# RWKV attention and a routed MoE on one core: the scan's inputs in three loads, asked for a chunk ahead, and scaled in place

## The chip, the cores and the metric

One core of a Trainium2 chip runs the whole program. A time is what one execution takes on the device, in microseconds (us); a verdict compares medians of several executions. The engines are TensorE (PE, with its weight loads as PEld), VectorE (DVE), ScalarE (ACT), GpSimd (POOL) and SyncE (SP). Each works through its own queue of instructions in order. SP issues nearly all DMAs here, and an instruction that waits holds up all that stand behind it in its queue.

## What is computed

Two stages, one fed by the other (shapes: batch 4, 8 heads, 768 steps, head size 40, float32):

```python
for t in range(768):                     # per batch and head
    y[t]  = r[t] @ state
    Sa    = state @ a[t]                 # state is 40x40
    state = state * w[t] - outer(Sa, b[t]) + outer(v[t], k[t])
x = y, 3072 tokens of 320 numbers
e = argmax(x @ w_gate); out = gate(e) * sigmoid(x @ w_output_gate)[e] * (relu(x @ w1[e]) @ w2[e])
```

## The kernel before, in words

The 768 steps are cut into 12 chunks of 64 steps. Within a chunk the recurrence is written as matrix products and the inverse of a triangular matrix, so that only the state goes from chunk to chunk. `Att` does the attention, `Moe` the experts.

For each chunk `c` four pieces of work follow each other:

- `scan(c)` (lines 98 to 119) loads `w` (371 KB) and `D`, which holds a, k and b side by side (1080 KB), and runs two scans on DVE that give products of decays, `P` and `I`. The scans read a constant of ones and zeros, `rst`, which POOL writes (lines 77 and 78). Then a reciprocal `rq` and the scaling of `I`.
- `prep(c)` (line 126): DVE scales a into `Av` (lines 173 and 174) and k, b into `KBt` (line 190). SP copies `Av` to two places in on-chip memory, to `Am` (line 180) and to strips of `LA` (line 167); three DMAs each, 330 KB together. PE multiplies `KBt` with `Am` into `pl` (line 203). ACT and DVE move `pl` to `N` and `LA`, and POOL masks `LA` (line 218). PE transposes `KBt` and `Wp` (line 152).
- `tinv` (line 227) inverts the triangular matrices on DVE: chunk 0 and chunk 1 alone, then two chunks at a time. Its first instruction reads `N` (lines 242, 247), its last gives `Tc` (lines 306, 312).
- `crit(c, q)` (line 343), for each half `q` of the heads, is the chain that carries the state: PE products `pa` with `XS`, `Tc`, `N`, with moves on ACT and additions on DVE between them. `tail(c, q)` gives the output `x`, which `route` stores (`xd`) and multiplies with the gate.

After chunks 3, 7, 10 and 11 `pick` chooses the experts, and POOL scatters the records (`tab`, line 695), each scatter behind the last. When chunk 7 is picked, the table is read back (`tr`, `tb`, line 804), tokens are gathered (`xg`, line 745) and transposed (`px`, line 753), and the first expert starts while the attention still runs. Afterwards the experts run alone: `ph` (line 776) and `po` (lines 789 to 791).

`run` (line 473) is a program order: `crit` in front, and after each of its steps four steps of a background generator, which does `prep`, `scan` of the next chunk and `tinv`. A scheduler then reorders the instructions of each engine by its own estimate of their times; `issue_after` says that what it encloses may not be placed before a given instruction. The order that it gives is fixed in the program. The tile names are the buffers: a tile of a pool with one buffer can be written again only when all that read it are done. `Av`, `KBt`, `D` and `w` have one buffer each. At the start, 56 products with zeros (`warm`, line 121) keep PE busy. They wait for `zb`, a constant that POOL writes.

## Time and profile before

| | us |
|---|---|
| median of 3 runs | 729.64 |
| the runs | 729.64, 733.31, 726.88 |
| the profiled execution, its time | 735.93 |
| its span, first to last instruction | 734.2 |

| engine | busy us in the span | share |
|---|---|---|
| PE | 651.8 | 89% |
| PEld | 582.8 | 79% |
| DVE | 470.2 | 64% |
| ACT | 339.8 | 46% |
| POOL | 208.7 | 28% |

The mean granted TensorE clock was 0.945 of full speed. The attention takes the time up to about 470 us, with the first expert mixed in from about 400 us on; the rest is the experts. The profiled execution stands 6.29 us above the median of the runs; durations are read from it and sums are made against its 735.93 us.

### The profile page before, as it was taken

What the parts mean: (1) busy time and instruction counts of PE and PEld (TensorE: products, weight loads), DVE (VectorE), ACT (ScalarE), POOL (GpSimd) and SP (SyncE); (2) the same over time, 40 slices, a digit from 0 to 9 for tenths busy, and PEclk for the clock granted to TensorE, in tenths of its full rate; (3) what the DMA queues carried; (4) which work ended last, traced back from release to release, by engine and by line L of the source; (5) the groups of instructions that cost most, each with busy time, mean ns of one, the idle gap of its engine ahead of it and who ended that gap; (6) DMA issues with size and microseconds to landing.
All of it is one profiled execution on the core that took longest, in us unless ns stands there. A gap on an engine that the chain in (4) does not pass through costs nothing.

```text
span 734.2 us, 21196 instructions
## 1 busy us (share of the span) xinstructions
PE 651.8 (89%) x8898; PEld 582.8 (79%) x8898; DVE 470.2 (64%) x914; ACT 339.8 (46%) x781; POOL 208.7 (28%) x316
## 2 busy tenths in 40 slices
PE   6768986898999999799998599788999999999994
PEld 5557875787987888688887488678999998988994
DVE  6678679868986898797796134453575544554230
ACT  2568662674477377347633144242465333433120
POOL 8442120330322246222112100243533231402111
PEclk9777899999999999999999599988999999999998
DMA  7865552276347538532333542065385633431001
GB/s 174 178 152 138 148 141 74 72 172 147 88 133 182 117 91 182 124 94 82 84 78 76 111 134 59 21 178 165 102 226 160 180 121 104 130 117 45 18 10 30
DMA packets 64387, 85.12 MB, mean 116 GB/s; under 512 B 34586, under 2 KB 51613, under 8 KB 62846
## 3 DMA queue, kind: packets, MB, share of 16 engines
q1 hardware_dynamic: 60446, 74.79, 40.4%
q0 software_dynamic: 3840, 8.91, 4.3%
q8 instruction: 72, 1.18, 0.7%
q14 instruction: 29, 0.24, 0.1%
HBM read 67.59 MB, written 8.96 MB: 104 GB/s over the span
## 4 chain that ended last, share of the span: by engine, by line
PE 61%; DVE 13%; DMA 12%; ACT 7%; issue 4%; POOL 2%; SPq 0%; POOLq 0%; DVEq 0%; ACTq 0%
PE ph L776 14%; PE pa L368 6%; PE pM L440 5%; PE po L791 5%; PE po L789 5%; PE po L790 5%; DMA D<-in_din_dram 5%; PE pS L406 3%; PE pt L152 3%; PE pY L456 3%; PE pl L203 3%; PE pY L455 2%; ACT N L214 2%; PE pa L355 2%; PE pxt L623 2%
## 5 line engine op out<-in xcount | busy, mean ns | idle before, releaser
L218 POOL TENSOR_SCALAR_AFFINE_SELECT LA<-LA 64x192 f32<-64x192 f32 x144 | 59.3, 441 | 88.7 <-ACT LA L216 85.9
L781 DVE SCALAR_TENSOR_TENSOR hl<-ph,hh 128x480 fp32r<-128x480 f32 (+1 forms) x76 | 41.8, 563 | 66.4 <-ACT hh L780 66.3
L776 PE MATMUL ph<-xh,w1h 128*128 128x480 f32 (+1 forms) x228 | 80.5, 357 | 1.9 <-DVE hl L781 1.3
L789 PE MATMUL po<-w2h,hh 128*120 128x320 f32 x256 | 79.2, 313 | 1.0 <-ACT hh L780 0.9
L776 PE MATMUL ph<-xl,w1h 128*128 128x480 f32 (+1 forms) x228 | 79.9, 353 | 0.0
L790 PE MATMUL po<-w2l,hh 128*120 128x320 f32 x256 | 78.2, 309 | 0.0
L780 ACT ACTIVATE hh<-ph 128x480 fp32r<-128x480 f32 (+1 forms) x76 | 36.7, 498 | 86.8 <-PE ph L776 86.8
L791 PE MATMUL po<-w2h,hl 128*120 128x320 f32 x256 | 75.9, 310 | 0.0
L794 POOL DMA_INDIRECT out_dram<-y,ti x32 | 33.1, 1035 | 131.8 <-DVE y L793 69.0
L359 ACT ACTIVATE As<-pa,hq 128x320 f32<-128x320 f32 x80 | 42.1, 527 | 57.1 <-PE pa L368 48.0
L203 PE MATMUL pl<-Am,KBt 120*128 120x192 f32 (+1 forms) x288 | 59.1, 338 | 9.6 <-ACT LA L216 6.1
L456 PE MATMUL pY<-KB,M 128*64 128x64 f32 (+1 forms) x768 | 55.6, 231 | 10.9 <-DVE M L444 10.9
L214 ACT ACTIVATE N<-pl 32x192 f32<-32x192 f32 (+1 forms) x138 | 51.6, 374 | 25.7 <-PE pl L203 12.0
L695 POOL DMA_INDIRECT tab<-rec,si x24 | 28.4, 1182 | 117.6 <-DVE rec L692 46.5
L368 PE MATMUL pa<-As,Tc 64*32 64x40 f32 x1792 | 52.0, 206 | 9.4 <-ACT As L359 6.2
L456 PEld LDWEIGHTS pY<-KB,M 128*64 128x64 f32 x768 | 48.9, 144 | 13.9 <-DVE M L444 11.5
L455 PE MATMUL pY<-Sd,R 128*64 128x64 f32 (+1 forms) x704 | 56.9, 234 | 0.3 <-DVE base L669 0.3
L368 PEld LDWEIGHTS pa<-As,Tc 64*32 64x32 f32 x1792 | 41.1, 113 | 19.9 <-ACT As L359 7.3
L203 PEld LDWEIGHTS pl<-Am,KBt 120*128 120x128 f32 x288 | 44.7, 197 | 15.1 <-ACT LA L216 9.2
L440 PE MATMUL pM<-R,VU 128*128 128x128 f32 x384 | 53.8, 293 | 1.5 <-ACT VU L432 1.4
L776 PE MATMUL ph<-xh,w1l 128*128 128x480 f32 (+1 forms) x152 | 53.7, 353 | 0.0
L455 PEld LDWEIGHTS pY<-Sd,R 128*64 128x64 f32 x704 | 47.4, 143 | 4.7 <-issue 1.7
(186 smaller groups left out, 1562.2 us busy)
## 6 DMA issues: line engine op xcount, KB each, us to landing
D<-in_din_dram SPq DMA_DIRECT2D x12, 1080.0 KB
st<-in_w_dram SPq DMA_DIRECT2D x16, 512.0 KB
st<-in_w_dram SPq DMA_DIRECT2D x16, 480.0 KB
XS<-in_vt_dram SPq DMA_DIRECT2D x24, 256.0 KB
XU<-in_vt_dram SPq DMA_DIRECT2D x24, 256.0 KB
VU<-in_vl_dram SPq DMA_DIRECT2D x24, 208.0 KB
w<-in_win_dram SPq DMA_DIRECT2D x12, 371.2 KB
st<-in_w_dram SPq DMA_DIRECT2D x16, 256.0 KB
```

Source lines behind the costliest of these rows:

```text
L203: nc.tensor.matmul(pl[:, i, 0:nj], KBt[:, 6 * side + g0 + i].rearrange("p n t -> p (n t)"), Am[:, g0 + i:g0 + i + 6 * nj - 5:6, 0:64], sta ...
L214: s.mark['n', c] = nc.scalar.activation(out=nn, in_=pn, func=AF.Copy, scale=-1.0).ins
L218: g.affine_select(out=la[:, :, i], in_=la[:, :, i], pattern=[[0, nj], [1, C]], base=0, channel_multiplier=-1, compare_op=ALU.is_gt, fill=0.0)
L359: nc.scalar.activation(out=x, in_=pa, func=AF.Copy, scale=s.hq[:, h:h + 1])
L368: nc.tensor.matmul(pa[o + w:o + w + 32, i], m(p)[o:o + 64], x[o:o + 64, i, :], start=start, stop=True, tile_position=(o, o + w), skip_grou ...
L440: nc.tensor.matmul(pM[:, i], VU[:, h0 + i].rearrange("p n t -> p (n t)"), R[:, :, h0 + i], start=True, stop=True)
L455: nc.tensor.matmul(o, R[:, side, i, :], Sf[:, 40 * i:40 * i + w], start=True, stop=False)
L456: nc.tensor.matmul(o, Ms[i // 4][:, i % 4, side, :], Kf[:, k:k + w], start=not c, stop=True)
L776: nc.tensor.matmul(ph, l, r, start=(i == 0), stop=(i == 7))
L789: nc.tensor.matmul(po, hh[f][:, ts_], w2h[:, f], start=(f == 0), stop=False)
L790: nc.tensor.matmul(po, hh[f][:, ts_], w2l[:, f], start=False, stop=False)
L791: nc.tensor.matmul(po, hl[f][:, ts_], w2h[:, f], start=False, stop=(f == 7))
```

## The change

The host lays a (padded from 64 to 66 columns) and k, b in two arrays, `ain` and `kin`, where there was one. `load_w`, `load_a` and `load_k` load `w` (two buffers), `a` (371 KB, one buffer) and `kb` (720 KB, two buffers). Chunk 0's loads are issued at the start; those of chunk c + 1 are written in `prep(c)`. `Av` and `KBt` are no tiles of their own any longer: the products overwrite `a` and `kb`. `rst` is written by DVE, and first. Chunk 1's scans may not be placed before the scaling of chunk 0's `kb`, and the loads of the state, the gate's weights and chunk 2's `w` may not be placed before chunk 0's copies to `Am`.

```diff
@@ -37,14 +37,16 @@
     wd = d3([w]).reshape(nch, 120, 12, C)
     win = np.zeros((nch, 120, 12, 2, 33), w.dtype)
     win[:, :, :, 0, 1:], win[:, :, :, 1, 1:] = wd[..., 32:], wd[..., 31::-1]
-    din = np.ascontiguousarray(d3([a, k, b]).transpose(0, 1, 2, 4, 5, 3, 6)).reshape(nch, 120, 12, 3, C)
+    ain = np.zeros((nch, 120, 12, C + 2), a.dtype)
+    ain[..., 0:C] = d3([a]).reshape(nch, 120, 12, C)
+    kin = np.ascontiguousarray(d3([k, b]).transpose(0, 1, 2, 4, 5, 3, 6)).reshape(nch, 120, 12, 2, C)
     tr = lambda x: x.reshape(2, 2, 8, nch, C, 40).transpose(3, 1, 0, 5, 2, 4)
     rl = np.ascontiguousarray(tr(r))
     vl = np.zeros((nch, 2, 104, 8, C), v.dtype)
     vl[:, :, 0:40], vl[:, :, 64:104] = tr(v)[:, :, 0], tr(v)[:, :, 1]
     vt = np.ascontiguousarray(v.reshape(2, 2, 8, nch, C, 40).transpose(3, 1, 4, 2, 0, 5))
     vt = np.concatenate([vt, np.zeros(vt.shape[:-1] + (24,), vt.dtype)], -1)
-    return win, din, rl, vl, vt
+    return win, ain, kin, rl, vl, vt
 
 
 def pat(x, off, dims):
@@ -55,9 +57,9 @@
 class Att:
     npool = 0
 
-    def __init__(s, ctx, tc, ident, win, din, rl, vl, vt, nch=12):
+    def __init__(s, ctx, tc, ident, win, ain, kin, rl, vl, vt, nch=12):
         s.tc, s.nc, s.nch, s.ident = tc, tc.nc, nch, ident
-        s.win, s.din, s.rl, s.vl, s.vt = win, din, rl, vl, vt
+        s.win, s.ain, s.kin, s.rl, s.vl, s.vt = win, ain, kin, rl, vl, vt
         nc = s.nc
         pool = lambda n, b, **k: ctx.enter_context(tc.tile_pool(name=n, bufs=b, **k))
         s.cp, s.p2, s.p5 = (pool(f"p{i}", i) for i in (1, 2, 5))
@@ -65,6 +67,9 @@
         s.dr = pool("dr", 2, space=DRAM)
         s.pre = ExitStack()
         s.p1 = s.pre.enter_context(tc.tile_pool(name="p0", bufs=1))
+        s.rst = s.p1.tile([120, 792], BF16, name="rst")
+        nc.vector.memset(s.rst, 0.0)
+        nc.vector.memset(s.rst[:, 0:792:33], 1.0)
         s.mM = s.cp.tile([128, C], F32, name="mM")
         nc.gpsimd.memset(s.mM, 1.0)
         for h in range(2):
@@ -73,9 +78,6 @@
 
         s.Am = s.p1.tile([120, 2, NP, 66], F32, name="Am")
         nc.gpsimd.memset(s.Am, 0.0)
-        s.rst = s.p1.tile([120, 792], BF16, name="rst")
-        nc.gpsimd.memset(s.rst, 0.0)
-        nc.gpsimd.memset(s.rst[:, 0:792:33], 1.0)
         s.Tt = s.p1.tile([128, 1056], F32, name="Tt")
         nc.gpsimd.memset(s.Tt, 0.0)
         nc.gpsimd.memset(s.Tt[:, 0:1056:33], 1.0)
@@ -92,21 +94,33 @@
         s.zb = s.cp.tile([128, 32], F32, name="zb")
         nc.gpsimd.memset(s.zb, 0.0)
         s.buffers()
+        s.w, s.a, s.kb = {}, {}, {}
         s.st, s.ld, s.post, s.idle, s.mark = {}, {}, [], False, {}
 
+
+    def load_w(s, c):
+        n = 12 * 2 * 33
+        w = s.w[c] = s.p1.tile([120, n + 1], F32, name="w", bufs=2)
+        s.nc.vector.memset(w[:, n:], 0.0)
+        with s.tc.issue_after(s.mark['am', 0]) if c == 2 else ExitStack():
+            s.nc.sync.dma_start(out=w[:, 0:n], in_=s.win[c])
+
+    def load_a(s, c):
+        s.a[c] = s.p1.tile([120, 12, 66], F32, name="a")
+        s.nc.sync.dma_start(out=s.a[c], in_=s.ain[c])
+
+    def load_k(s, c):
+        s.kb[c] = s.p1.tile([120, 12, 2, C], F32, name="kb", bufs=2)
+        s.mark[c] = s.nc.sync.dma_start(out=s.kb[c], in_=s.kin[c]).ins
 
     def scan(s, c):
 
         nc, V = s.nc, s.nc.vector
         n = 12 * 2 * 33
-        w = s.p1.tile([120, n + 1], F32, name="w")
-        V.memset(w[:, n:], 0.0)
-        nc.sync.dma_start(out=w[:, 0:n], in_=s.win[c])
-        s.D = s.p1.tile([120, 12, 3, C], F32, name="D")
-        s.mark[c] = nc.sync.dma_start(out=s.D, in_=s.din[c]).ins
+        w = s.w.pop(c)
         P, I = (s.p1.tile([120, 12, 2, 33], F32, name=x) for x in "PI")
         Pf, If = (x.rearrange("p r h t -> p (r h t)") for x in (P, I))
-        with s.tc.issue_after(s.mark['t', 0]) if c == 2 else ExitStack():
+        with s.tc.issue_after(s.mark['t', 0] if c == 2 else s.mark['k', 0]) if c in (1, 2) else ExitStack():
             for o, d in ((Pf, w[:, 0:n]), (If[:, ::-1], w[:, n:0:-1])):
                 V.tensor_tensor_scan(out=o, data0=d, data1=s.rst, initial=0.0, op0=ALU.mult, op1=ALU.add)
         wq = pat(w, 1, [(33, 24), (1, 32)])
@@ -129,8 +143,12 @@
         g, V = nc.gpsimd, nc.vector
         st = s.st[c] = {}
         P, I, rq = s.Q
-        D = s.D
-        yield
+        a, kb = s.a.pop(c), s.kb.pop(c)
+        Av = a
+        yield
+        if c + 1 < s.nch:
+            s.load_w(c + 1)
+            s.load_k(c + 1)
         LA = st["LA"] = s.p5.tile([128, 2, NP, 66], F32, name='LA', bufs=4)
         if c:
             g.memset(LA[32:64], 0.0)
@@ -142,7 +160,6 @@
         st['Np'] = s.Np
         for h in range(2):
             g.memset(N[64 * h + 32:64 * h + 64, :, 32:64], 0.0)
-        Av = s.p1.tile([120, 12, 66], F32, name="Av")
         Wp = s.p1.tile([120, 6, 2, C], F32, name="Wp")
 
         def back(dst, src):
@@ -168,7 +185,6 @@
 
         rs = s.p1.tile([120, 24], F32, name="rs", bufs=2)
         nc.scalar.activation(out=rs, in_=rq, func=AF.Square, accum_out=s.rqm[:, c:c + 1])
-        a, kb = D[:, :, 0], D[:, :, 1:3]
         with s.tc.issue_after(s.mark['r', 0]) if c == 1 else ExitStack():
             V.tensor_tensor(out=Av[:, :, 0:33], in0=a[:, :, 0:33], in1=I[:, :, 1, ::-1], op=ALU.mult)
             V.tensor_tensor(out=Av[:, :, 33:64], in0=a[:, :, 33:64], in1=P[:, :, 0, 1:32], op=ALU.mult)
@@ -177,18 +193,20 @@
         Ag = Av.rearrange("p (a g) t -> p a g t", a=2)
         for j in range(3):
             r, n = slice(40 * j, 40 * j + 40), 6 if j < 2 else 4
-            am = nc.sync.dma_start(out=s.Am[r, :, 6 * j:6 * j + n], in_=Ag[r, :, 0:n]).ins
+            am = s.mark['am', c] = nc.sync.dma_start(out=s.Am[r, :, 6 * j:6 * j + n], in_=Ag[r, :, 0:n]).ins
         if c:
             with s.tc.issue_after(am):
                 strips()
         else:
             s.later = strips
         yield
-        KBt = s.p1.tile([120, 12, 2, C], F32, name="KBt")
+        if c + 1 < s.nch:
+            s.load_a(c + 1)
+        KBt = kb
         with s.tc.issue_after(s.mark['r', 0]) if c == 1 else ExitStack():
             for h, d in ((0, P[:, :, 1, 31::-1]), (32, I[:, :, 0, 1:33])):
-                V.tensor_tensor(out=KBt[:, :, :, h:h + 32], in0=kb[:, :, :, h:h + 32],
-                                in1=d.unsqueeze(2).broadcast_to([120, 12, 2, 32]), op=ALU.mult)
+                s.mark['k', c] = V.tensor_tensor(out=KBt[:, :, :, h:h + 32], in0=kb[:, :, :, h:h + 32],
+                                                 in1=d.unsqueeze(2).broadcast_to([120, 12, 2, 32]), op=ALU.mult).ins
         yield
         for h, n, d in ((0, 33, I[:, :, 1, ::-1]), (33, 31, P[:, :, 0, 1:32])):
             nc.scalar.copy(out=pat(Wp, h, [(C, 2), (2 * C, 6), (1, n)]), in_=d.rearrange("p (a g) t -> p a g t", a=2))
@@ -493,11 +511,15 @@
 
         def background():
             s.warm(s.ident, 56)
+            s.load_w(0)
+            s.load_a(0)
+            s.load_k(0)
             s.scan(0)
             for b in batches:
                 yield from preps(b)
                 if b == batches[0]:
-                    first()
+                    with s.tc.issue_after(s.mark['am', 0]):
+                        first()
                 yield from inv(b)
             s.pre.close()
             s.idle = True
@@ -514,9 +536,10 @@
             while c not in ready:
                 next(bg)
         need(0)
-        s.load_r(0, 0)
-        s.load_x(0, 0)
-        s.load_x(0, 1)
+        with s.tc.issue_after(s.mark['am', 0]):
+            s.load_x(0, 0)
+            s.load_x(0, 1)
+            s.load_r(0, 0)
         tail = iter(())
 
         def later(k):
...
```

The parts left out pass the two arrays through.

The scheduler places instructions anew on all engines. Three places matter below.

SP, from the load of chunk 2's `w` to the load of chunk 3's `w` (`Am`, `LA`: the copies of chunk 1; `D`, `a`, `kb`: inputs of chunk 2; `XS`: values for chunks 1 and 2). Before:

```order
L104 DMA w<-in_win_dram 120x792
L180 DMA Am<-Av 40x2x396 x2
L180 DMA Am<-Av 40x2x264
L167 DMA LA<-Av 40x2x396 x2
L167 DMA LA<-Av 40x2x264
L106 DMA D<-in_din_dram 120x2304
L338 DMA XS_147<-in_vt_dram 64x1024
L338 DMA XS_151<-in_vt_dram 64x1024
L104 DMA w<-in_win_dram 120x792
```

And with the change:

```order
L106 DMA w<-in_win_dram 120x792
L114 DMA kb<-in_kin_dram 120x1536
L106 DMA w<-in_win_dram 120x792
L196 DMA Am<-a 40x2x396 x2
L196 DMA Am<-a 40x2x264
L184 DMA LA<-a 40x2x396 x2
L184 DMA LA<-a 40x2x264
L356 DMA XS_147<-in_vt_dram 64x1024
L356 DMA XS_151<-in_vt_dram 64x1024
L110 DMA a<-in_ain_dram 120x792
```

Chunk 2's `kb` and chunk 3's `w` have moved ahead of chunk 1's copies; chunk 2's `a` has to stand behind them, because they read the one buffer that it fills.

DVE, from the scans of chunk 2 to the first additions of `crit(0, 0)` (L381, L399: `As`). Before:

```order
L111 SCALAR_TENSOR_TENSOR P<-w,rst 120x792
L111 SCALAR_TENSOR_TENSOR I<-w,rst 120x792
L116 RECIPROCAL rq<-P 120x24
L174 TENSOR_TENSOR Av<-D,P 120x12x31
L118 TENSOR_TENSOR I<-I,rq 120x792
L173 TENSOR_TENSOR Av<-D,I 120x12x33
L103 MEMSET w 120x1
L381 TENSOR_TENSOR As<-As,pa 32x320 x2
```

And with the change:

```order
L125 SCALAR_TENSOR_TENSOR P<-w,rst 120x792
L125 SCALAR_TENSOR_TENSOR I<-w,rst 120x792
L130 RECIPROCAL rq<-P 120x24
L208 TENSOR_TENSOR kb<-kb,P 120x24x32
L190 TENSOR_TENSOR a<-a,P 120x12x31
L132 TENSOR_TENSOR I<-I,rq 120x792
L104 MEMSET w 120x1
L189 TENSOR_TENSOR a<-a,I 120x12x33
L208 TENSOR_TENSOR kb<-kb,I 120x24x32
L399 TENSOR_TENSOR As<-As,pa 32x320 x2
```

The scaling of `kb`, which came after a part of `tinv` before, now stands with that of `a`.

DVE, where the first expert starts (L804, L827: the table read back; L411, L429: the state after chunk 9, 10; L444, L462: `M` of `tail`). Before:

```order
L411 TENSOR_TENSOR XS_147<-tmS,Dt 40x8x40
L458 TENSOR_TENSOR x<-pY,WT 128x320
L410 TENSOR_TENSOR tmS<-XS_151,pS 40x320
L725 TENSOR_TENSOR w1l<-st,w1h 128x1024
L411 TENSOR_TENSOR XS_147<-tmS,Dt 40x8x40
L804 COPY tb<-tr 120x128
L806 CAST ti<-tb 120x64
L444 TENSOR_TENSOR M<-pM,mM 128x512 x2
```

And with the change:

```order
L429 TENSOR_TENSOR XS_147<-tmS,Dt 40x8x40
L462 TENSOR_TENSOR M<-pM,mM 128x512
L748 TENSOR_TENSOR w1l<-st,w1h 128x1024
L462 TENSOR_TENSOR M<-pM,mM 128x512
L827 COPY tb<-tr 120x128
L829 CAST ti<-tb 120x64
L476 TENSOR_TENSOR x<-pY,WT 128x320
```

Two `M` now stand ahead of the table's copy and no longer behind it. On PE, 21 more products `pa<-XS,LA`, 40 more `pa` of the solve, 11 more `pS` and 29 more `pY` stand between the last product of chunk 7's `pick` and the first `px` than before.

## Rows read from the trace of the kernel before

**Rows 1.** The page's part 1: busy us, share and instructions of each engine.

```profile
PE 651.8 (89%) x8898; PEld 582.8 (79%) x8898; DVE 470.2 (64%) x914; ACT 339.8 (46%) x781; POOL 208.7 (28%) x316
```

**Rows 2.** Waits of DVE up to 400 us: total us, times, longest.

```profile
DVE Av L174 <- DMA D<-in_din_dram: 11.5, 5, 4.7
DVE Av L173 <- DMA w<-in_win_dram: 4.6, 1, 4.6
DVE Av L173 <- DMA XS<-in_vt_dram: 2.1, 1, 2.1
DVE Av L174 <- DMA VU<-in_vl_dram: 2.0, 1, 2.0
```

**Rows 3.** Timeline of PE: start, us, what; in brackets idle before and releaser.

```profile
111.93 0.55 PE L619 MATMUL pxt<-ident,x 128*128 128x128 f32 x3 [1.03 <-DVE w L103]
...
178.63 0.90 PE L619 MATMUL pxt<-ident,x 128*128 128x128 f32 x3 [2.17 <-DVE x L458]
...
240.61 2.05 PE L440 MATMUL pM<-R,VU 128*128 128x128 f32 x16 [0.60 <-ACT VU L432]
...
245.21 0.27 PE L456 MATMUL pY<-KB,M 128*64 128x64 f32 x1 [0.79 <-DVE M L444]
...
311.25 0.27 PE L456 MATMUL pY<-KB,M 128*64 128x64 f32 x1 [4.26 <-DVE M L444]
```

**Rows 4.** Timeline of the start: the warm-up, chunk 0's first scan, its first products.

```profile
6.64 14.71 PE L124 MATMUL fl<-ident,zb 128*32 128x128 f32 x112 [6.64 <-POOL zb L93]
...
11.35 1.81 DVE L111 TENSOR_TENSOR_SCAN P<-w,rst 120x792 f32<-120x792 f32 x1 [3.82 <-POOL rst L78]
...
22.27 3.29 PE L203 MATMUL pl<-Am,KBt 120*128 120x192 f32 x20 [0.91 <-DMA Am<-Av]
```

**Rows 5.** Chain of work that ended last: start, us from issue to landing.

```profile
20.54 8.07 DMA D<-in_din_dram
28.62 6.61 DMA XU<-in_vt_dram
...
41.57 8.99 DMA D<-in_din_dram
```

**Rows 6.** Timeline of SP: issue, us to issue, what.

```profile
32.84 0.34 SPq L104 DMA_DIRECT2D w<-in_win_dram  x1
...
36.43 2.54 SPq L180 DMA_DIRECT2D Am<-Av  x3
...
298.33 2.45 SPq L167 DMA_DIRECT2D LA<-Av  x3
300.88 0.45 SPq L106 DMA_DIRECT2D D<-in_din_dram  x1
```

**Rows 7.** Timeline: chunk 1's first products, and chunk 2's first scaling.

```profile
40.80 4.25 PE L203 MATMUL pl<-Am,KBt 120*128 120x192 f32 x12 [1.82 <-DVE Yt L295]
...
50.88 0.62 DVE L174 TENSOR_TENSOR Av<-D,P 120x372 f32<-120x372 f32 x1 [4.01 <-DMA D<-in_din_dram]
```

**Rows 8.** Timeline of the first expert's start: scatters, table, transposed tokens.

```profile
375.66 1.01 POOL L695 DMA_INDIRECT tab<-rec,si  x1 [20.10 <-DVE M L444]
...
403.62 0.97 POOL L695 DMA_INDIRECT tab<-rec,si  x1 [1.40 <-DMA tab<-rec,si]
...
410.87 0.27 DVE L804 COPY tb<-tr 120x128 f32<-120x128 f32 x1 [9.11 <-DMA tr<-tab]
...
418.18 0.66 PE L753 MATMUL px<-ident,xg 120*128 120x120 f32 x2 [5.67 <-DMA xg<-xd,ti]
```

**Rows 9.** Timeline of PE: products of `crit` at the full clock.

```profile
358.37 0.89 PE L355 MATMUL pa<-XS,LA 128*64 128x64 f32 x24
...
386.29 0.79 PE L406 MATMUL pS<-XU,KB 128*40 128x40 f32 x16
387.00 0.76 PE L368 MATMUL pa<-As,N 64*32 64x40 f32 x32
```

**Rows 10.** Busy us of the engines by stretch, then granted clock, DMA share, GB/s.

```profile
410.00:420.00 10.00, 2.30 (x24) 1.73 (x24) 2.42 (x5) 1.48 (x2) 2.24 (x2) 0.54 0.76 183
```

More of the change, by code (lines that the diff above doesn't have):

```diff
@@ L998, in moe, with rwkv_moe_kernel @@
                 nc.sync.dma_start(out=s.out[bass.ds(i * 128, 128), :], in_=acc)
-def rwkv_moe_kernel(tc, win, din, rl, vl, vt, r, k, v, w, a, b, wg, wo, w1, w2, out, nch=12):
+def rwkv_moe_kernel(tc, win, ain, kin, rl, vl, vt, r, k, v, w, a, b, wg, wo, w1, w2, out, nch=12):
     nc = tc.nc
@@ L1011, in rwkv_moe_kernel @@
             with ExitStack() as c2:
-                att = Att(c2, tc, ident, win, din, rl, vl, vt, nch=nch)
+                att = Att(c2, tc, ident, win, ain, kin, rl, vl, vt, nch=nch)
                 ps = lambda sh, nm, tag="tl", n=3: lambda *_: att.ps.tile(sh, F32, name=nm, tag=tag, bufs=n)
@@ L1039 @@
 _OUT = ((3072, 320), 'float32')
-_LAY = ('win', 'din', 'rl', 'vl', 'vt', 'r', 'k', 'v', 'w', 'a', 'b')
+_LAY = ('win', 'ain', 'kin', 'rl', 'vl', 'vt', 'r', 'k', 'v', 'w', 'a', 'b')
 def lay_all(*raw):
```

## The prediction

> **What bounds the kernel now.** I read the page's totals first. TensorE is busy for 651.8 of 734.2 us, DVE for 470.2 [rows 1]. The change removes no product and no vector operation worth counting, so it can win only time in which TensorE stands idle: 734.2 - 651.8 = 82 us in all. The next view is the list of waits on DVE: the scaling of a chunk's a waits for DMAs, 11.5 us in five waits put down to `D`, and 4.6, 2.1 and 2.0 us put down to loads issued near it, 20.2 us together [rows 2]. The third is the timeline of TensorE, to see which of these waits reach it. Five idle pieces lie behind a late scaling: 1.03, 2.17, 0.60, 0.79 and 4.26 us [rows 3]. They are the small share of the DVE waits that TensorE pays for; the others fall where TensorE had other work. The last is the start and the chain: `D` is on the chain of waits for 8.07 and 8.99 us [rows 5].
>
> **The start.** Chunk 0's first scan waited 3.82 us for `rst` [rows 4]; DVE was free at 7.5 us. With `rst` written first by DVE the scan starts some 3 us sooner. What hides the gain is the warm-up: it stands ahead of chunk 0's `pl` on TensorE and ends at 6.64 + 14.71 = 21.35 us, and `pl` starts at 22.27 with 0.91 us of waiting for the copy to `Am` [rows 4]. So 0.9 us is about all there is. The queue can take that back. The rate of a full queue: when chunk 1's `D` landed (28.61), 330 KB of `LA`, 160 of `R`, 208 of `VU` and 256 each of `XS` and `XU` were behind it, and `XU` landed 6.61 us later [rows 5]: 1210 KB, 183 KB/us. With the change w, a, kb, w, kb, XS, XU, R and VU (371 + 371 + 720 + 371 + 720 + 256 + 256 + 160 + 208 = 3433 KB) are issued before chunk 0's `Am`; at 183 that is 18.8 us, and `Am` lands near 22 as before. Term: 0, bounds -0.9 and +2.
>
> **Chunk 1's copies.** Here the change costs something. Chunk 1's `Am` was issued at 36.43, with `w` (32.84) as the fresh load ahead of it [rows 6], and the products that read it began at 40.80, after 1.82 us of idling [rows 7]. Six of these products stand ahead of the first solve of `crit(0, 0)` on TensorE in both orders. Now `kb` of chunk 2 and `w` of chunk 3 stand ahead as well: 1091 KB, at 183 KB/us 6.0 us, so `pl` of chunk 1 starts near 46.8. Behind it, `a` of chunk 2 waits on SP until the strips of `LA` have landed, since they read its buffer: 46.8 + 330 KB (1.8) = 48.6, then 512 KB of `XS` (2.8) and `a` itself (2.0): 53.4. Before, the scaling came at 50.88, after 4.01 us of waiting for `D` [rows 7]. The wait that should go is replaced by a longer one: +2.5 us for the additions of `crit` and the `tinv` of chunk 1, which stand behind it on DVE. I take +2.5 and not 6.0, because DVE's wait is what ends last there. Lower bound 0 (the queue is drained sooner); upper bound +8.1, at the rate of `D` alone, 1080 KB in 8.07 us or 134 KB/us [rows 5].
>
> **The later chunks.** `kb` and `w` are there a chunk ahead. `a` is not: it is asked when the strips of the chunk before have landed. But that is 701 KB after the copies instead of 1080 KB after the scaling of `KBt`, and it comes sooner. Where the two scans and a part of `tinv` lie between, the wait goes. The worst place is the last chunk: strips issued until 300.78 [rows 6], landed and `a` loaded at 134 KB/us: 306.1. The scaling stood until 309.4 after 4.7 us [rows 2], so 3.2 of 4.7 goes and 1.4 of TensorE's 4.26 us stays. Term: 1.03 + 2.17 + 0.60 + 0.79 + 4.26 = 8.85 [rows 3], less 1.4: -7.5. Bounds: 0, and -11.2 if half of the 7.4 us of DVE waits that TensorE does not show (20.2 - 8.85 - 4.0) comes back, too, where DVE is busiest. The scalings in place are the same instructions on other addresses: 0.
>
> By the Trainium skill's page "DMA: Bandwidth & Descriptors" (Anatomy of one DMA) every DMA has a fixed price of about 2 us, most of it the confirmation of the last byte; paid one after another by the 12 loads that come from splitting `D`, that is an estimate of 24 us, and 746 in the end. The rows: eight transfers with all their bytes landed within 6.61 us [rows 5], 0.83 us each at the most, so no such price is paid in turn here.
>
> **The first expert's start.** Eight scatters run from 375.66 to 403.62, each behind the last, then the table returns (410.87) and TensorE gets its tokens at 418.18, after 5.67 us of waiting [rows 8]; in that stretch it was busy for 2.30 of 10 us at a granted clock of 0.54, near the lower of its two levels [rows 10]. The length of this chain is not touched. The new order puts more products between `pick` and the first `px`: 21 at 0.037, 11 at 0.049 and 40 at 0.024 us [rows 9], and 29 `pY`, for which I take 0.024. That is 0.78 + 0.54 + 0.96 + 0.70 = 3.0 us of work that fills the wait: -3.0, bounds -4.5 (the higher clock) and 0. Next late there is the table's copy on DVE, with the next state's `tmS` behind it.
>
> **Sum.** 0 + 2.5 - 7.5 - 3.0 = -8.0 us. From the profiled execution's 735.93 that is 727.9; that execution lies 6.29 above the median of the runs, 729.64, so the forecast is **721.6**, its own range 716 to 728.
>
> **The rivals.**
>
> More comes back: the queue is drained sooner at the start (0 instead of +2.5), and the DVE waits that TensorE does not show shorten the stretches where DVE is the limit (-3.7). -14.2: 715.4. For it speaks the wait of 4.6 us right before a `tinv` of two chunks; against it, that TensorE lost little there. Chance 0.23.
>
> The same: the delay of chunk 1's copies reaches the chain in full (+6.0), and the first expert's start keeps its length, because the scatters set it, not the work beside them. 6.0 - 7.5 = -1.5: 728.1. For it speaks that TensorE has 82 us of idle in many small pieces, so that a wait removed can come back at the next. In the same case lies a price for each further load, paid in turn, at the most that the rows allow: 12 x 0.83 = +9.9 on the forecast, 731.5 (0.03). Chance 0.27 together. (That price is the rule of the Trainium skill named above.)
>
> Slower: one buffer for `a` with the deep queue. If the queue moves 134 KB/us, as `D` alone did, chunk 1's copies come 8.1 us late. And every later chunk pays strips and load one after the other, 330 + 371 KB or 5.2 us, as long as the waits that are removed, so the steady gain is gone. +8.1: 737.7. It decides if `pl` of chunk 1 starts after 48 us and DVE's waits for `a` still sum to 15 us or more. For it speaks that `a` is requested a chunk ahead in the code only, not in the order; against it, that the scans of the next chunk mostly come long after the strips. Chance 0.15.
>
> The forecast keeps 0.35, of which I put 0.22 below 722.3.
>
> **The numbers.** A measurement of this kernel, whose runs lie between 726.88 and 733.31, can tell about 1%, 7.3 us, from no change. Faster by more than that: 0.23 + 0.22 = 0.45. Within it: 0.13 + 0.27 = 0.40. Slower: 0.15. The range 712 to 736 leaves out most of the slower case (0.13) and 0.05 below.
>
> **What would show it.** Right: chunk 0's first scan before 9 us and its `pl` still at 21 to 23; `pl` of chunk 1 at 45 to 48; a DVE wait for `a` of chunk 2 that ends at 52 to 54; later waits of the scaling below 6 us in all; TensorE's idle of 4.26 us near 311 below 2. Wrong: `pl` of chunk 1 at 41 or earlier, or later than 49; DVE waits for `a` as long as those for `D`; or TensorE's idle time from 20 to 470 us unchanged although those waits are gone. Then something else ends the idle pieces, and the sum over [rows 3] was not mine to take.

## The result and the profile after

The changed kernel takes **738.62 us** (median of 20 runs, 730.68 to 748.31) against 729.82 (20 runs, 724.59 to 735.9): ratio **1.009**, interval 1.0062 to 1.0118. The ratios, and all medians from here on, leave out runs that took over 1.5% more than the fastest of their kernel: 8 of the 20 here, whose median without them is 736.37, and one of the 20 before (729.64). The medians of these counted runs differ by 6.7 us. The profiled execution took 739.16 us, 2.8 above that median; that of before lay 6.3 above its own.

The page's part 1 of the changed kernel, against [rows 1]:

```profile
span 737.4 us, 21168 instructions
...
PE 658.1 (89%) x8898; PEld 587.8 (80%) x8898; DVE 472.4 (64%) x916; ACT 339.6 (46%) x781; POOL 213.2 (29%) x314
```

TensorE's idle time went from 82.4 us to 737.4 - 658.1 = 79.3. Its busy time rose by 6.3 us for the same 8898 matmuls, at a mean granted clock of 0.929 against 0.945. But a second profile of the kernel before (e0) has 76.5 us idle and 656.5 busy, so one pair of profiles settles neither. The timed runs are clearer: the median granted clock is 0.937 here, 0.949 in 100 runs of the kernel before. Within either kernel a run with 0.01 less of it is longer, by 4.2 us (before) or 3.3 (after), a straight line through the runs. For 0.012 that makes 4 to 5 us, an estimate, of the 6.7 between the medians. Such a line shows that clock and time go together, not which comes first.

**The start**, against [rows 4], in the timelines of TensorE and VectorE:

```profile
5.96 15.09 PE L138 MATMUL fl<-ident,zb 128*32 128x128 f32 x112 [5.96 <-POOL zb L95]
...
6.69 1.80 DVE L125 TENSOR_TENSOR_SCAN P<-w,rst 120x792 f32<-120x792 f32 x1
...
20.98 3.32 PE L221 MATMUL pl<-Am,kb 120*128 120x192 f32 x20
```

The scan is 4.7 us sooner, `pl` 1.3 us sooner, behind the warm-up without a wait.

**Chunk 1's copies.** SP's timeline (`w` and `kb` of later chunks, then `Am` of chunk 1, then `a` of chunk 2), and what follows on TensorE, ScalarE and VectorE, against [rows 6, 7]:

```profile
30.36 0.53 SPq L106 DMA_DIRECT2D w<-in_win_dram  x1
30.99 0.33 SPq L114 DMA_DIRECT2D kb<-in_kin_dram  x1
31.43 0.35 SPq L106 DMA_DIRECT2D w<-in_win_dram  x1
32.72 2.52 SPq L196 DMA_DIRECT2D Am<-a  x3
...
47.41 0.34 SPq L110 DMA_DIRECT2D a<-in_ain_dram  x1
```

```profile
45.11 4.15 PE L221 MATMUL pl<-Am,kb 120*128 120x192 f32 x12 [9.37 <-DMA Am<-a]
...
46.77 0.82 ACT L232 ACTIVATE N<-pl 32x384 f32<-32x384 f32 x2 [11.53 <-PE pl L221]
48.11 0.91 ACT L327 ACTIVATE Tc<-tmpf,hm 128x256 f32<-128x256 f32 x2
...
51.26 0.55 DVE L190 TENSOR_TENSOR a<-a,P 120x372 f32<-120x372 f32 x1 [7.27 <-DMA a<-in_ain_dram]
```

The same two copies on ScalarE in the kernel before:

```profile
42.46 0.82 ACT L214 ACTIVATE N<-pl 32x384 f32<-32x384 f32 x2 [3.97 <-PE pl L203]
43.80 0.91 ACT L309 ACTIVATE Tc<-tmpf,hm 128x256 f32<-128x256 f32 x2
```

In both orders ScalarE has `N` of chunk 1 ahead of `Tc` of chunk 0, and `N` needs the `pl` that waits for the late copy. So `Tc`, without which no solve begins, is copied 4.3 us later, though chunk 0's inverse began 3.6 us sooner. The first `XU` is written at 72.5 instead of 68.0.

**The waits**, against [rows 2]: VectorE's up to 400 us (total, times, longest), and SP's from 20 to 400.

```profile
DVE a L190 <- DMA a<-in_ain_dram: 11.7, 3, 7.3
...
DVE kb L208 <- DMA kb<-in_kin_dram: 6.1, 3, 3.4
```

```profile
SPq L110 <- DMA LA<-a: 25.3, 17, 5.7
```

`a` is waited for as long as `D` was, since SP asks for it only when the copies to `LA` have landed. VectorE's three waits for it, near 51, 183 and 252 us, each stand behind such a standstill. By the Trainium skill's page "DMA: Bandwidth & Descriptors" (Anatomy of one DMA) a DMA's wait is served on the issuing sequencer before dispatch; the row agrees, and all that is queued behind stands too. That this costs time is not shown by the row (e2 below).

**Near 300 us**, where before TensorE idled 4.26 us [rows 3]: SP, VectorE, TensorE, and the busy time of the engines by stretch (window, then its length; the granted clock is the third number from the right).

```profile
286.67 0.34 SPq L110 DMA_DIRECT2D a<-in_ain_dram  x1
287.07 0.56 SPq L357 DMA_DIRECT2D XU<-in_vt_dram  x1
287.67 0.59 SPq L356 DMA_DIRECT2D XS<-in_vt_dram  x1
288.31 0.90 SPq L352 DMA_DIRECT2D VU<-in_vl_dram  x1
289.25 0.60 SPq L114 DMA_DIRECT2D kb<-in_kin_dram  x1
...
299.66 0.96 DVE L208 TENSOR_TENSOR kb<-kb,P 120x768 f32<-120x768 f32 x1 [3.44 <-DMA kb<-in_kin_dram]
...
301.43 0.48 DVE L476 TENSOR_TENSOR x<-pY,WT 128x320 f32<-128x320 f32 x1
...
301.97 0.90 PE L642 MATMUL pxt<-ident,x 128*128 128x128 f32 x3 [2.09 <-DVE x L476]
...
317.70 1.13 PE L458 MATMUL pM<-R,VU 128*128 128x128 f32 x4
```

```profile
300.00:302.00 2.00, 0.03 (x1) 0.03 (x1) 2.00 (x4) 1.93 (x5) 1.93 (x3) 0.91 0.00 0
302.00:318.00 16.00, 16.00 (x119) 13.45 (x120) 7.38 (x17) 4.92 (x13) 2.29 (x5) 0.50 0.36 110
```

Chunk 10's `kb` comes 3.4 us late, `x` stands behind it on VectorE, TensorE pauses for 2.1 us, and then runs for 16 us at the lower level: a clock of 0.50, 119 matmuls. The load of `kb` stands behind `XU`, `XS` and `VU` in SP's queue; SP's wait for `a`, just ahead of them, was 0.3 us here. The 121 matmuls from this `pxt` to the last row of the timeline took 16.9 us.

**The first expert's start**, against [rows 8]:

```profile
386.04 1.02 POOL L718 DMA_INDIRECT tab<-rec,si  x1 [11.69 <-DVE Yt L316]
...
412.74 0.97 POOL L718 DMA_INDIRECT tab<-rec,si  x1 [2.44 <-DMA tab<-rec,si]
...
426.43 0.42 PE L776 MATMUL px<-ident,xg 120*128 120x120 f32 x2 [3.35 <-DMA xg<-xd,ti]
```

The scatters begin 10.4 us later than before and the tokens are there 8.3 us later; the wait is 2.3 us shorter.

### The profile page after: what moved, and what is told of

Same layout as the page of the kernel before. It is cut to its first block, busy times and chain, and to the rows that moved or that the text cites. A ratio compares the mean times of both kernels' runs of the same rounds, so it can differ in the third digit from the quotient of the medians.

```text
span 737.4 us, 21168 instructions
## 1 busy us (share of the span) xinstructions
PE 658.1 (89%) x8898; PEld 587.8 (80%) x8898; DVE 472.4 (64%) x916; ACT 339.6 (46%) x781; POOL 213.2 (29%) x314
## 4 chain that ended last, share of the span: by engine, by line
PE 59%; DMA 12%; DVE 12%; ACT 8%; issue 4%; POOL 3%; SPq 0%; POOLq 0%; ACTq 0%; DVEq 0%
PE ph L799 14%; PE pa L386 5%; PE pM L458 5%; PE po L814 5%; PE po L812 5%; PE po L813 5%; DMA LA<-a 3%; PE pS L424 3%; ACT N L232 3%; PE pt L169 3%; PE pxt L646 3%; DMA kb<-in_kin_dram 2%; PE pY L474 2%; ACT LA L234 2%; PE pY L473 2%
## 5 line engine op out<-in xcount | busy, mean ns | idle before, releaser
L804 DVE SCALAR_TENSOR_TENSOR hl<-ph,hh 128x480 fp32r<-128x480 f32 (+1 forms) x76 | 41.7, 562 | 66.1 <-ACT hh L803 63.6
L236 POOL TENSOR_SCALAR_AFFINE_SELECT LA<-LA 64x192 f32<-64x192 f32 x144 | 61.6, 457 | 61.2 <-ACT LA L234 59.4
L221 PE MATMUL pl<-Am,kb 120*128 120x192 f32 (+1 forms) x288 | 61.7, 345 | 14.7 <-DMA Am<-a 9.4
L817 POOL DMA_INDIRECT out_dram<-y,ti x32 | 35.3, 1102 | 134.4 <-DVE y L816 75.1
L458 PE MATMUL pM<-R,VU 128*128 128x128 f32 x384 | 59.6, 313 | 7.4 <-ACT VU L450 7.3
L221 PEld LDWEIGHTS pl<-Am,kb 120*128 120x128 f32 x288 | 45.5, 200 | 20.3 <-issue 9.7
L458 PEld LDWEIGHTS pM<-R,VU 128*128 128x128 f32 x384 | 53.4, 219 | 9.4 <-ACT VU L450 8.0
L474 PE MATMUL pY<-KB,M 128*64 128x64 f32 (+1 forms) x768 | 54.1, 226 | 1.1 <-DVE M L462 1.0
L473 PE MATMUL pY<-Sd,R 128*64 128x64 f32 (+1 forms) x704 | 54.4, 229 | 0.2 <-issue 0.2
L386 PE MATMUL pa<-As,Tc 64*32 64x40 f32 x1792 | 50.5, 205 | 3.4 <-ACT As L377 3.2
L799 PEld LDWEIGHTS ph<-xh,w1h 128*128 128x128 f32 x228 | 44.5, 197 | 8.4 <-ACT xh L778 2.3
```

The lines of the kernel that those rows point to most:

```text
L221: nc.tensor.matmul(pl[:, i, 0:nj], KBt[:, 6 * side + g0 + i].rearrange("p n t -> p (n t)"), Am[:, g0 + i:g0 + i + 6 * nj - 5:6, 0:64], sta ...
L236: g.affine_select(out=la[:, :, i], in_=la[:, :, i], pattern=[[0, nj], [1, C]], base=0, channel_multiplier=-1, compare_op=ALU.is_gt, fill=0.0)
L386: nc.tensor.matmul(pa[o + w:o + w + 32, i], m(p)[o:o + 64], x[o:o + 64, i, :], start=start, stop=True, tile_position=(o, o + w), skip_grou ...
L458: nc.tensor.matmul(pM[:, i], VU[:, h0 + i].rearrange("p n t -> p (n t)"), R[:, :, h0 + i], start=True, stop=True)
L473: nc.tensor.matmul(o, R[:, side, i, :], Sf[:, 40 * i:40 * i + w], start=True, stop=False)
L474: nc.tensor.matmul(o, Ms[i // 4][:, i % 4, side, :], Kf[:, k:k + w], start=not c, stop=True)
```

## The experiments

Us and clock are medians of the counted timed runs; waits are VectorE's waits for DMAs from 20 to 400 us, us in all, in the profiled execution.

| run | us | ratio to before (interval) | clock | waits |
|---|---|---|---|---|
| before, e0 | 729.74 | 1.0015 (0.9979-1.0051) | 0.950 | 21.9 |
| after | 736.37 | 1.009 (1.0062-1.0118) | 0.937 | 17.8 |
| e1 w, k/b behind the copies | 733.38 | 1.0034 (0.9997-1.0071) | 0.933 | 14.0 |
| e2 two a, one w | 719.60 | 0.9837 (0.9786-0.9888) | 0.951 | 10.6 |
| e3 both | 731.09 | 0.9988 (0.9948-1.0027) | 0.938 | 21.1 |
| e4 one a, one w | 740.62 | 1.0153 (1.01-1.0207) | 0.931 | 17.7 |
| e5 scaled a over w | 739.71 | 1.0165 (1.011-1.022) | 0.934 | 30.1 |
| e6 constants alone | 731.13 | 1.0049 (1.001-1.0088) | 0.941 | 25.1 |
| e7 two a, early loads first | 722.17 | 0.9914 (0.9878-0.995) | 0.953 | 11.9 |
| e8 k/b of chunk 10 first | 736.08 | 1.0105 (1.0044-1.0166) | 0.942 | 16.7 |
| e9 copies of chunk 1 first | 740.16 | 1.0107 (1.0053-1.0161) | 0.935 | 15.7 |
| e10 e5 without the memset | 732.75 | 1.003 (0.9993-1.0068) | 0.937 | 3.0 |
| e11 e8 and e9 | 729.41 | 0.9968 (0.9927-1.0009) | 0.945 | 14.1 |
| e12 e2 without the memset | 719.30 | 0.9883 (0.9848-0.9919) | 0.949 | 9.2 |
| e13 two of each | 765.87 | 1.051 (1.0476-1.0544) | 0.919 | 43.3 |
| e14 e2 and e9 | 721.72 | 0.9897 (0.9861-0.9933) | 0.944 | 12.1 |
| e15 e13 and e9 | 765.25 | 1.0468 (1.0412-1.0523) | 0.912 | 44.9 |
| e16 two a, asked behind LA | 723.45 | 0.9946 (0.9909-0.9984) | 0.944 | 10.2 |

**e0_before.** No edit.

> The kernel before, run against itself, for the spread of the measurement and for the granted clock of its runs. Clock theory (the lost time is TensorE work at the lower level): the granted clock of its runs lies near that of its one profile, 0.945, and above the 0.924 to 0.948 (middle 0.936) of the changed kernel's runs. Queue theory and buffer theory (the lost time is waiting for transfers) say nothing of the clock: it may be the same. Time 727 to 733 us, ratio 1 within 0.004.

As expected in time. Its profile (span 733.0, clock 0.938) shows 656.5 us of busy TensorE where the other profile of the same kernel shows 651.8, so the medians of the clock decide, and those differ. The idle pieces differ as well. The largest of [rows 3], 4.26 us, is this here:

```profile
311.92 0.27 PE L456 MATMUL pY<-KB,M 128*64 128x64 f32 x1 [0.98 <-DVE M L444]
```

The same five matmuls have 0.87, 1.57, 0.60, 0.33 and 0.98 us of idle time before them, 4.35 in all and not 8.85.

**e1_kbw_behind.**

```diff
-        if c + 1 < s.nch:
+        if c == 0:
             s.load_w(c + 1)
             s.load_k(c + 1)
...
             with s.tc.issue_after(am):
                 strips()
+                if c + 1 < s.nch:
+                    s.load_w(c + 1)
+                    s.load_k(c + 1)
```

> The changed kernel, with w and k/b of chunk c+1 asked for behind chunk c's copies of the scaled a (from chunk 1 on), not ahead of them. Queue theory (k/b and two w, 1.45 MB, stand ahead of chunk 1's copies in the queue; at 183 KB/us 8 us): pl of chunk 1 starts at 38 to 41 us, not 45.1; TensorE idles there below 5 us, not 9.4; chunk 0's Tc is copied by 44 us, not 48.1; 733 to 735 us. Buffer theory (the one buffer of a lets each load of a wait for the landing of the copies to LA, and holds up SP): later loads of a still wait, 736 to 740 us. Clock theory: the time follows the granted clock, whatever becomes of the wait at 45 us.

In time as the queue theory had it, 3 us below the changed kernel; the first `XU` is written at 68.1, the waits for `a` fall to 0.4 us, against the buffer theory, though SP still stands for the copies to `LA` for 18.2 us. But the waits for `kb` and `w` rise to 13.6, and the clock stays low. What is saved at one load is waited for at the next.

**e2_two_a.**

```diff
-        w = s.w[c] = s.p1.tile([120, n + 1], F32, name="w", bufs=2)
+        w = s.w[c] = s.p1.tile([120, n + 1], F32, name="w")
...
-        s.a[c] = s.p1.tile([120, 12, 66], F32, name="a")
+        s.a[c] = s.p1.tile([120, 12, 66], F32, name="a", bufs=2)
```

> The changed kernel with two buffers for a, in exchange for one instead of two for w (there is no room for both). Buffer theory: VectorE's waits for a fall from 11.7 us to below 4, SP no longer stands still before the loads of a, PE's waits for VU, XU and x shrink, 731 to 734 us. Queue theory: pl of chunk 1 still starts at 43 us or later, and the time stays at 736 to 740 us. If w's one buffer costs as much as the second of a gains, VectorE's waits move from a to w.

17 us below the changed kernel, 1.6% below the kernel before. VectorE's waits for DMAs, SP's for the copies to `LA`, and the first expert's start:

```profile
DVE P L125 <- DMA w<-in_win_dram: 6.9, 1, 6.9
...
DVE kb L208 <- DMA kb<-in_kin_dram: 3.3, 2, 2.3
...
SPq L110 <- DMA LA<-a: 21.9, 13, 5.3
```

```profile
361.52 1.01 POOL L718 DMA_INDIRECT tab<-rec,si  x1 [9.49 <-DVE tmpf L308]
...
408.06 0.66 PE L776 MATMUL px<-ident,xg 120*128 120x120 f32 x2 [7.62 <-DMA xg<-xd,ti]
```

`a` is not waited for at all, though SP stands nearly as long as before: with two buffers the load that waits for the copies is one of a later chunk. TensorE's first 3400 matmuls come in the changed kernel's order; they are through at 241.5 us, not 251.5, so at least these 10 us come from the transfers and not from another order on TensorE. Behind them 1908 of its 8898 rows are in another place. The tokens are there at 408, not 426.

**e3_both.** Both edits.

> Both edits: w and k/b of the chunk after behind the copies of the scaled a, and two buffers for a with one for w. If queue and buffer each cost their own share, 727 to 731 us, the sum of what the two edits give one by one. Queue theory alone: as the first edit alone, 733 to 735. Buffer theory alone: as the second alone, 731 to 734. If it stays at 736 or more, the waits that both take away were not what the end hung on.

None of the theories: the two do not add, the second buffer's gain is gone. With `w` and `kb` asked for late, VectorE waits 21.1 us for these two. All three loads have to be early; e10 shows that this alone is not enough.

**e4_one_w.** The first half of e2's diff alone.

> The changed kernel with one buffer for w and still one for a: the half of the experiment e2_two_a that was only the price of the second a. Buffer theory (a's second buffer made the gain): VectorE still waits for a 8 us or more in all, 736 to 742 us. Order theory (any edit deals the scheduler's order anew, and e2_two_a drew a good one; or the queue is eased because a second w no longer stands ahead of chunk 1's copies): waits for a stay, yet the time falls to 731 us or below.

Against the order theory: 740.6. Between this and e2 lies only the second buffer of `a`: 21 us. The waits here:

```profile
DVE a L190 <- DMA a<-in_ain_dram: 5.0, 2, 4.3
...
SPq L110 <- DMA LA<-a: 27.0, 21, 5.5
```

TensorE's order is the changed kernel's except for some 20 rows, so against e2 it differs behind the first 3400 matmuls; they are through at 250.8 us, 9 of the 21 us later than in e2.

**e5_av_in_w.**

```diff
-        w = s.w.pop(c)
+        w = s.w[c]
...
-        Av = a
+        Av = s.w.pop(c)[:, 0:792].rearrange("p (r t) -> p r t", r=12)
```

> The changed kernel with the scaled a written over chunk c's w (793 words a partition, free after the scan and the Square) and not over a: a is read once and is free when the scaling is done, and both w and k/b keep their second buffer. Buffer theory: a is asked for right after the scaling, not after the landing of the copies to LA; VectorE's waits for a below 4 us in all; 716 to 725 us, as with two buffers of a. Order theory: an edit like any other, anywhere between 720 and 742, with no tie to the waits for a.

A miss, and VectorE's waits show a reason:

```profile
DVE w L104 <- DMA LA<-w: 21.6, 8, 4.0
```

The memset of the next `w`'s last column, one element a partition, now waits for the copies to `LA`, and VectorE behind it. SP, too, still stands for them, 22.1 us, before it asks for `w`.

**e6_rst_alone.** The kernel before, `rst` set first, by VectorE.

> The kernel before with the scan constants written first on VectorE, and nothing else of the change. What the start is worth by itself: scan before 9 us, pl of chunk 0 at 21 to 22 us behind the warm-up; 727 to 731 us, not to be told from 730. Order theory: it may go anywhere between 722 and 738, though hardly anything is moved.

No gain, rather a loss of 0.5%. The scan starts at 6.7 us as expected, `pl` at 24.2 and not at 21 to 22: it waits 3.7 us for its copies. And 3412 of TensorE's 8898 rows are in another place, so this is no clean price of the start.

**e7_two_a_no_defer.** e2, and:

```diff
-                    with s.tc.issue_after(s.mark['am', 0]):
-                        first()
+                    first()
...
-        with s.tc.issue_after(s.mark['am', 0]):
-            s.load_x(0, 0)
-            s.load_x(0, 1)
-            s.load_r(0, 0)
+        s.load_x(0, 0)
+        s.load_x(0, 1)
+        s.load_r(0, 0)
```

> The changed kernel with two buffers for a and one for w, and without the rule that holds back the first loads of XS, XU, R, VU, G and tab until chunk 0's copies of the scaled a are asked for. Queue theory: those 1.4 MB then stand ahead of chunk 0's copies, which start is hidden by the warm-up, and no longer ahead of chunk 1's: pl of chunk 1 starts below 40 us, and the time is 2 to 5 us below e2_two_a's 719.6, 715 to 718. If what stands ahead of chunk 1's copies costs nothing, 718 to 722.

Nothing gained, and TensorE still waited 7.1 us for `Am`. The gain of the second `a` stays with the loads in another order (722.2); TensorE's order is e2's except for some 40 rows.

**e8_kb_ahead.** Three rows of SP's queue moved, no other row on any engine:

```diff
-                            if c + 1 < n:
+                        with s.tc.issue_after(s.mark[10] if c == 6 and 10 in s.mark else s.mark[1]):
+                            if c + 1 < n:
                                 s.load_x(c + 1, q)
```

> The changed kernel with one move in SP's queue: XS and XU of chunk 7 and one more XS (768 KB, 4.2 us at 183 KB/us) behind the load of chunk 10's k/b, not ahead of it. Nothing else is in another place, on any engine. In the changed kernel VectorE waits 3.4 us for this k/b at 296 us, TensorE stands still 2.1 us at 300 behind it, and then runs 17 us at the lower level. Place theory (one late load, with x behind it on VectorE, starts the low stretch): the wait is below 1.5 us, the low stretch at 300 is at most 3.4 us, and the time falls by 2 + 7 = 9 us to 728 to 732. Buffer theory: the wait for a before each chunk is what counts; 736 to 740, no change. Clock theory without a place (the level falls by chance): the low stretch stays or turns up elsewhere, 734 to 740.

Split. The profiled execution (728.53 us) does what the place theory said; the same stretch:

```profile
298.15 0.96 DVE L208 TENSOR_TENSOR kb<-kb,P 120x768 f32<-120x768 f32 x1 [1.45 <-DMA kb<-in_kin_dram]
...
300.61 0.55 PE L643 MATMUL pxt<-ident,x 128*128 128x128 f32 x3 [0.25 <-DVE x L476]
...
309.81 0.65 PE L458 MATMUL pM<-R,VU 128*128 128x128 f32 x4
```

```profile
302.00:318.00 16.00, 15.98 (x282) 13.73 (x279) 13.23 (x28) 8.70 (x24) 4.14 (x9) 1.00 0.65 162
```

282 matmuls in the window instead of 119, but it begins further on in the order. The same 121 matmuls took 9.9 us here and 16.9 in the changed kernel: the low stretch cost 7 us, and 8 us of the lead are left when the tokens come (418.3 against 426.4). But the other three counted runs took 733.4 to 739.2 us, at clocks from 0.947 down to 0.935, and the median is where it was. So one pause had 7 us of slow matmuls behind it in one execution; removing this place does not lower the median. That the median loss hangs on this place alone is refuted.

**e9_am_ahead.** e1's diff for chunk 1 alone: `kb` and one `w` of chunk 2 behind its copies.

> The changed kernel with chunk 1's three copies of the scaled a ahead of chunk 2's k/b and one of the two w (1.1 MB, 6.1 us), and else only a few rows of chunk 2 moved. Queue theory: pl of chunk 1 starts near 39 to 41 us, not 45.1, chunk 0's Tc is copied by 44 us and not 48.1, the first XU is written 4 us sooner (68.5, not 72.5), and as nothing behind it is moved the end comes 3 to 5 us sooner: 733 to 736. If something else holds that place, TensorE's idle 9.4 us turns into a wait for Tc or N and the time stays at 738.

The place as expected, the end not:

```profile
40.48 4.00 PE L224 MATMUL pl<-Am,kb 120*128 120x192 f32 x12 [4.32 <-DMA Am<-a]
...
43.48 0.91 ACT L330 ACTIVATE Tc<-tmpf,hm 128x256 f32<-128x256 f32 x2
...
426.21 0.66 PE L779 MATMUL px<-ident,xg 120*128 120x120 f32 x2 [8.42 <-DMA xg<-xd,ti]
```

Until 407 us TensorE runs 5 us ahead of the changed kernel; the tokens come at 426.21 against 426.43, and the 5 us turn into a longer wait for them.

**e10_av_in_w_pad.** e5, with `w`'s last column in the input and the memset gone.

> The experiment e5_av_in_w once more, with w's last column loaded with the rest (a zero column in the input) and no longer set by VectorE. There VectorE waited 21.6 us with that one-column memset for the landing of the copies to LA. Buffer theory (the scaled a apart from a is worth as much as a second a, and the memset took it away): VectorE's waits for LA are gone, 716 to 726 us. If the time stays above 735, it is not the free a that made the gain of e2_two_a.

7 us from the memset, as e5 suggested (TensorE's order is e5's except for some 40 rows), but not e2's level, though VectorE waits for 3.0 us only. Its order differs from e2's, on TensorE in 3270 rows. So VectorE's waits for loads are not the whole account.

**e11_both_places.** e8 and e9 together.

> The moves of e8_kb_ahead and e9_am_ahead together; a has one buffer as in the changed kernel. Place theory and queue theory: the gains add, 738 - 9 - 4 = 725 to 729 us, below the kernel before. Buffer theory: 733 to 738, since a still has one buffer.

7 us below the changed kernel, level with the kernel before, though e8 and e9 gave nothing singly. So the whole loss against the kernel before goes when these two places are mended, with one buffer for `a`: that goes against the buffer theory as the only account. Why they count together and not singly is open.

**e12_two_a_pad.** e2 without the memset.

> e2_two_a again (a in two buffers, w in one), with w's last column loaded and not set by VectorE; SP's order and a few dozen rows of VectorE and TensorE are dealt anew. Buffer theory (a asked for a chunk ahead is what made e2_two_a fast): 716 to 724 us, as e2_two_a's 719.6 and e7_two_a_no_defer's 722.2. Order theory (the scheduler's order of e2_two_a was a lucky one): back toward 730 or more.

Buffer theory: 719.3, the lowest median, 1.2% below the kernel before. TensorE's order is e2's, so the order theory is not tested. The run has the 12 further loads of the change. By the Trainium skill's page "DMA: Bandwidth & Descriptors" (Anatomy of one DMA) a DMA that GpSimd issues has a fixed price of about 2 us; SP issues these loads. Paid one by one, that price would make an estimate of 24 us for them; the run, below the kernel before, shows no such sum.

**e13_full.**

```diff
-        s.a[c] = s.p1.tile([120, 12, 66], F32, name="a")
+        s.a[c] = s.p1.tile([120, 12, 66], F32, name="a", bufs=2)
...
-        Wp = s.p1.tile([120, 6, 2, C], F32, name="Wp")
+        Wp = s.w.pop(c)[:, 0:768].rearrange("p (g n t) -> p g n t", g=6, n=2)
```

> The changed kernel with a, w and k/b all in two buffers; the room comes from Wp, which is written over chunk c's w, and w's last column is loaded. Its order differs from e2_two_a's on every engine by hundreds of rows. Buffer theory: all loads a chunk ahead, VectorE's waits for loads below 5 us, 714 to 723 us. Order theory: anywhere from 720 to 740.

The largest miss: 766.

```profile
DVE P L125 <- DMA w<-in_win_dram: 43.3, 10, 11.6
```

`w` has two buffers here, too, but each is in use until `Wp` is transposed at the end of its chunk, and the load comes too late for the scan. The number of buffers says nothing without the last reader of each.

**e14_two_a_am_ahead, e15_full_am_ahead.** e9's edit on e2 and on e13.

> e2_two_a with chunk 1's copies of the scaled a ahead of chunk 2's k/b and w in SP's queue, and no other row moved on any engine. Queue theory (1.1 MB ahead of these copies, 6.1 us at 183 KB/us, hold ScalarE's queue and with it chunk 0's Tc): pl of chunk 1 starts at 39 to 40 us, not 43.0, the first XU is written 2 to 3 us sooner, and the time falls to 716 to 718. If chunk 2's k/b and w then come late, the gain is lost by the second chunk: 719 to 724.

> e13_full with chunk 1's copies of the scaled a ahead of chunk 2's k/b and w. Queue theory: 2 to 3 us below e13_full. Otherwise as e13_full within 2 us.

`pl` of chunk 1 starts at 40.8 in e14 (42.97 in e2), and the end gains nothing; no more does e15's (38.7 against 44.5 in e13). Without e8's move the late copies of chunk 1 cost nothing that stays.

**e16_two_a_behind_la.** e2, and:

```diff
+            with s.tc.issue_after(s.mark['la', c]) if c else ExitStack():
+                s.load_a(c + 1)
```

> e2_two_a with each load of a (from chunk 2's on) held in SP's queue behind the copies to LA of the chunk before, the place that it has in the changed kernel; it need not wait for their landing, since it has a buffer of its own. Buffer theory, asked early (what made e2_two_a fast is that a is asked for a whole chunk ahead): 732 to 741 us, as with one buffer. Buffer theory, no standstill (what made it fast is that SP no longer waits for the landing of those copies before it goes on): 717 to 724 us. Order theory: the order of TensorE differs from e2_two_a's in some hundred rows, so anywhere.

By its range no standstill: 723.5, 17 of the 21 us between e4 and e2. The load stands behind the copies as in the changed kernel, SP asks at once, and no wait for `a` is left:

```profile
38.31 2.39 SPq L184 DMA_DIRECT2D LA<-a  x3
40.75 0.51 SPq L110 DMA_DIRECT2D a<-in_ain_dram  x1
```

But the theory took it that in e2 SP does not stand for the copies, and there it does, 21.9 us. So the two runs differ in the standstill, and what they share is that `a` is there when VectorE wants it. On TensorE this order is not e2's (1121 rows elsewhere) and nearer to the changed kernel's (458), so the gain is not the luck of e2's order.

## Why the prediction was wrong

Forecast were 8.0 us less; the counted runs took 6.7 us more.

**The start** (0): right. Scan at 6.7, `pl` at 21.0.

**Chunk 1's copies** (+2.5): the mechanism was right, `pl` at 45.1 in the 45 to 48 foreseen, the wait for chunk 2's `a` ending at 51.3. Its price was not: what ended last there was not VectorE's wait but ScalarE's queue, `N` ahead of `Tc`, +4.3 there. Yet at the end of the program it is worth nothing by itself (e9; e14 moved it by 2 us only), and 7 us together with the place near 300 us (e11).

**The later chunks** (-7.5): the step that failed. It said that `a` "comes sooner" than `D` because only 701 KB stand between the copies and it. But with one buffer SP cannot ask for `a` before those copies have landed, 25.3 us in 17 waits, and VectorE waited 11.7 us for it, as long as for `D`: one of the prediction's own signs of being wrong. The later waits by the scaling were 10.5 us, 4.4 for `a` and 6.1 for `kb`, where below 6 had been foreseen. Shown by e4, e2 and e16: with a buffer of its own for the next `a` the same change takes 719.6 and 723.5, with one 740.6. The cause is not the standstill as such, since e2 has 21.9 us of it; what the traces of e2 and e16 share is that the load which stands, or comes late, is not the one that VectorE wants next. That reading is not tested by itself, and e10, with no wait for `a`, shows that it is not the whole. And `kb` near 300 us was late because of what stood ahead of it in the queue (e8), not because of `a`.

The size of the term was doubtful as well. Its 8.85 us of idle pieces come from one execution; in e0, the same kernel, they are 4.35. TensorE's idle time from 20 to 470 us was 54.1 and 47.3 us in the two profiles of before and 52.2 after: unchanged, another of the prediction's signs.

**The price of a pause.** The sum counted TensorE's idle pieces at their length and the matmuls at one clock. In the pair of profiles the pieces summed to 3.1 us less, and the matmuls took 6.3 us more; 2.09 us of idle at 300 came, with 17 us at half the clock behind it, which cost 7. The granted clock is higher with two `a` (0.944 to 0.953, in e2, e7, e12, e14 and e16) than with one in e4 (0.931). It does not follow VectorE's waits alone: the kernel before has 0.950 with 21.9 us of them, e10 0.937 with 3.0. Which pauses set the low level off is open, as e8 shows.

**The first expert's start** (-3.0): the wait for tokens is 2.3 us shorter in this pair, near the forecast, but by luck: the same order on TensorE, but for some 20 rows, waits 3.75 us in e8, 6.65 in e4 and 8.42 in e9, against 5.67 and 5.05 in the two profiles of before. So the products that the order puts ahead do not set it. e9 shows its other side: time won before it is lost in it.

**The rivals.** The slower case named the one buffer of `a`, with copies and load paid one after the other, and 737.7 us, near the result. That the steady gain would be gone was right. The number was in part luck: its two marks (`pl` after 48 us, 15 us of waits for `a`) did not come, it reckoned with a slower queue, and it left out the -3.0 of the first expert without a reason.

Open is why e10, with the fewest waits for loads, is not as fast as e2, why the two places count only together (e11), and how much of e2's gain behind the first 3400 matmuls belongs to the order that the scheduler dealt.

## What to carry to other kernels

A load is ahead only if its buffer is free: find the last reader of each buffer, copies out of it included, before believing in a prefetch, and mind that scaling in place makes that reader a later one. The wait of a load stands on the queue that issues it; ask which engine wants that load, and what is behind it, and how soon. On VectorE a one-column memset of a reused tile is such a wait, too. Price a pause of TensorE by the clock after it as well as by its length, and read an idle piece in two profiles before it goes into a sum.

## What the runs showed of the hardware

After a pause of 2.1 us TensorE ran 16 us at a granted clock of 0.50; the 121 matmuls behind the pause took 16.9 us, and 9.9 in another program with the same order, at 1.00 (e8). Four runs of one program (e8) spread from 728.5 to 739.2 us, at mean granted clocks from 0.947 to 0.935.
